# A fused attention and mixture-of-experts kernel: softmax sums turned in the products' PSUM bank, gathers released one by one, PSUM tiles for expert 0's pieces, and another order of ScalarE's copies

## The chip, the cores and the metric

The kernel runs on one core of a Trainium2 chip. Its time is the device time of one execution in microseconds, as the median of three runs. A profile of one more execution, taken by the hardware profiler, shows when each engine was busy and what it waited for.

## What is computed

Banded causal attention, whose output is at once the input of a layer of eight experts, of which each token uses one. All data is float32. Cut to what matters:

```python
B, H, S, D = 4, 8, 768, 64;  n_global, n_local = 8, 96
N, E, F = 3072, 8, 1024                     # tokens, experts, hidden size
scores = (q @ k.T) / sqrt(D) - slope[h] * dist    # dist: n_local for global keys outside the band
keep = (key < n_global) | ((0 <= query - key) & (query - key < n_local))
a = softmax(where(keep, scores, -1e9));  x = (a @ v) -> [3072, 512]
logits = x @ w_gate;  expert = argmax(logits);  gate = softmax(logits)[expert]
h = relu(x @ w1[expert]);  out = gate * (h @ w2[expert])   # 512 -> 1024 -> 512
```

## The kernel before

Each engine executes its instructions in the order in which the code calls them, and the instructions of different engines meet through semaphores. So the order of the calls in the loop at L803 is the schedule: if an instruction waits, everything behind it on its engine waits as well.

**Attention** (banded_attention, L370). The work is cut into 48 units: batch b, pair of heads j and a third c of the sequence, which is two blocks of 128 queries. A batch has 12 units. The loop at L803 takes two units in each step. scores (L486) multiplies blocks of 64 x 128 of the keys with the queries (L497) into a PSUM tile s of two banks; the keys of the block itself come from kT, and those of the block before it, with the eight global keys put in front, from kA. ScalarE takes the exponential (L503), and VectorE multiplies by a table of weights W that holds bias and mask (L510 for c = 0, L514 otherwise). One step later attend (L520) forms the products with v (L531) in the bank o_all; ScalarE copies them to w2_f (L534), and TensorE then forms the column sums of the exponentials with vectors of ones in the bank c_all (L553). Two steps after the scores turn (L556) transposes the products into px (L561), and ScalarE copies them into rows xr of the tokens (L566).

**PSUM.** The eight banks are handed out as follows: ps_s has two tiles of two banks (the scores), ps_o one bank (po_all, named o_all), ps_m two banks (tag m, everything small), ps_c one bank (pc_all, named c_all). A tile whose pool is full has to wait for the readers of the tile it takes the place of.

**For each pair of heads.** turn_qk (L448) transposes k and q on VectorE. keys_at (L419) makes kA with two ScalarE copies (L420, L422); the loop calls it at the end of the step of unit c = 1 for the next pair. turn_v (L441) makes va with two ScalarE copies (L444, L445); the loop calls it after unit c = 2, for the next pair. load and load_v start the DMAs some pairs ahead.

**For each batch, when its 12 units are through.** In the first step of the next batch (m = 0): sums_out (L572) copies the column sums to sums (L573), and partials (L586) forms partial logits for each pair of heads with products not yet divided by the sums (pl L592, ScalarE copy L594). In the second step (m = 2): recip_of (L575) transposes the sums (L578), adds them (two VectorE reductions, L581) and takes the reciprocals (L584); then logits (L596) transposes the partial logits into pq (L605, two tiles), and VectorE scales them by the reciprocals (L608), adds them over the heads and computes the gates. recip_of needs room in PSUM for the transposed sums: the loop takes the tile of the step's second unit early and puts them into its unused columns (the first lines below). In later steps spread (L628) ranks the tokens of each expert (VectorE, many small operations), finish_x (L620) multiplies the rows by the reciprocals (L624) and stores them to x_tok in DRAM (L245), tables (L657) builds one-hot tables (mv L662, oh L667), and spread_sum (L671) turns them into the lists of tokens by expert (pi L676). For batch 2, the last that is worked on inside the loop, all of this is packed into the steps m = 4 and m = 6.

```python
if b > 0 and n0 % nb == 2 and n == n0:
    st["ps"] = ps_s.tile([P, 2, 512], F32, tag="s", name=f"s_{n + 1}")
    recip_of(b - 1, st["ps"][:, :, 3 * P:4 * P])
...
if i == 0:
    while pending:
        gather_one(*pending.pop(0))
```

**Hand-over to expert 0.** Expert 0 starts before the last batch is finished, with 256 of its tokens from batches 0 to 2. half_0 (L684) prepares their list. fetch_0(0) (L693), called before the products of the last but one step, turns the list into rows (a matmul pw in rows_of, L263) and queues eight gathers on GpSimd (gather_one, L281, an indirect DMA of 32 rows each), all at once (the last lines above). Behind the loop (L858 on) comes a list written out by hand: sums, partial logits, logits, rows and tables of batch 3, with pieces of expert 0 in between (work, L726): early_hidden (L715, hidden_0: ph L339, relu L341) and early_result (L718, result_0: po L347, scaled by the gates into y on VectorE, L327). All early_hidden pieces share the two halves of one tile ph of ps_s, all early_result pieces the two halves of another, po. The half of ph that is not in use at first also holds the transposed sums of the last batch. turn_x (L289) transposes the gathered rows of a token block into xe on VectorE.

pace (L308) is the means by which gathers are spread over the experts' work: it takes the next gather from the list pending and makes it wait for a given instruction.

**Experts.** From L1198 on, hidden (L1115) and result (L1170) go through the experts: ph L1125, relu L1127, po L1182, then y L327 and an indirect DMA to the output. Weights come by SyncE's DMAs while the expert before is worked on.

Of the kernel before, what the change touches and what calls it, by code (L numbers as in the profile page):

```python
# [29 lines left out]
def kernel(  # L30
# [339 lines left out]
    def banded_attention():  # L370
        with ExitStack() as actx:
# [114 lines left out]
            def scores(n):  # L486
# [4 lines left out]
                ps = st.pop("ps") if "ps" in st else ps_s.tile([P, 2, 512], F32, tag="s", name=f"s_{n}")  # L491
# [11 lines left out]
                nc.scalar.activation(e[:, :, 0:w], ps[:, :, 0:w], AF.Exp, scale=D ** -0.5)  # L503
# [16 lines left out]
            def attend(*ns):  # L520

                for n in ns:
# [3 lines left out]
                    for t in range(2):  # L526
                        mine = [(m, own) for m, (u, own) in enumerate(bl) if u == t]
                        for m, own in mine:
                            i = 2 * c + t
                            for h in range(2):  # L530
# [3 lines left out]
                nc.scalar.copy(out=w2_f[:, o:o + 2 * P * len(ns)],  # L534
                               in_=po_all[:, ns[0] % 2:ns[-1] % 2 + 1, :, :].rearrange("p n t q -> p (n t q)"))
                for n in ns:
# [5 lines left out]
                    for own in (1, 0):  # L542

                        lots = [(1, 2)] if c == 0 and not own else [(0, 1), (1, 2)] if m == 1 and not own else [(0, 2)]
                        for t0, t1 in lots:
                            for h in range(2):
# [3 lines left out]
                                else:  # L550
# [3 lines left out]
                                                 start=(m == 0), stop=(m == nb - 1))  # L554

            def turn(n):  # L556
# [5 lines left out]
                for i in range(2):  # L562
# [3 lines left out]
                    nc.scalar.copy(out=xrs[b, c][:, :, P * j:P * j + P], in_=px[:, 2 * i:2 * i + 2, :])  # L566
# [8 lines left out]
            def recip_of(b, pr):  # L575

                for t in range(2):
                    nc.tensor.transpose(pr[:, t, :], sums[:, t, :], ident)  # L578
# [114 lines left out]
            def fetch_0(i):  # L693
# [6 lines left out]
                if i == 0:  # L700
                    while pending:
                        gather_one(*pending.pop(0))
                else:
                    for _ in range(2):
                        gather_one(*pending.pop(0))
                    plan(1)
# [8 lines left out]
            def early_hidden(z, f0):  # L715
                return hidden_0(st["ph"][:, f0 // 2 % 2, 0:2 * P], z, f0, 2)

            def early_result(z, f0):  # L718
                return result_0(st["po"][:, z, :], z, f0, 2, later)
# [76 lines left out]
            weights(0)  # L796
            nu = len(units)
# [5 lines left out]
            for n0 in range(0, nu, 2):  # L803
# [5 lines left out]
                for n in two:  # L809
# [8 lines left out]
                    if b > 0 and n0 % nb == 2 and n == n0:  # L818

                        st["ps"] = ps_s.tile([P, 2, 512], F32, tag="s", name=f"s_{n + 1}")  # L820
                        recip_of(b - 1, st["ps"][:, :, 3 * P:4 * P])
# [6 lines left out]
                if n0 >= 4:  # L828
                    turn(n0 - 4)
                    if b > 0 and m == 2:  # L830
                        logits(b - 1)
                    if n0 == nu - 4:
                        fetch_0(0)
                    attend(n0 - 2, n0 - 1)
                if b > 0 and m == 0:
                    sums_out(b - 1)
                    partials(b - 1)
                if b > 0 and m == 4:
                    spread(b - 1)
                if b > 0 and m == (4 if b == B - 1 else 8):  # L840
                    for i in range(NB // 2):
                        finish_x(b - 1, i)
                if 0 < b and m == (4 if b == B - 1 else 6):
                    tables(b - 1)
# [435 lines left out]
```

## Time and profile before

| | before |
|---|---|
| device time, three runs | 534.8, 536.1, 540.2 us |
| median | 536.09 us |
| the profiled execution | 538.75 us, span of the instructions 537.0 us |
| mean granted clock of TensorE in it | 0.985 of full speed |
| gathers (L281, xq) of expert 0 | 15, 1052 ns each |
| scores (L497) | 704 matmuls, 40.1 + 34.9 us |
| exponentials (L503) written to the tiles e | 36, 946 ns each |

The page of the profile gives the busy time and the number of instructions of each engine first: PE is the matrix multiplication of TensorE, PEld its load of weights, which overlaps with PE, DVE VectorE, ACT ScalarE, POOL GpSimd. Views of the trace answer closer questions: the waits of an engine (what it waited for, and who ended the wait), windows (busy time of each engine in a stretch of time), and the timeline (each instruction with its start, its duration, and in brackets the idle time of its engine before it and who ended that). In a timeline "s<-qT,kT" names the output tile and the inputs, "128x1024 f32" the partitions and elements, "x4" that four like instructions follow one another. An idle time in brackets ended by "remote" was ended by a semaphore whose sender the profile doesn't name.

### The profile page before, as it was taken

What the parts mean: (1) busy time and instruction counts of PE and PEld (TensorE: products, weight loads), DVE (VectorE), ACT (ScalarE), POOL (GpSimd) and SP (SyncE); (2) the same over time, 40 slices, a digit from 0 to 9 for tenths busy, and PEclk for the clock granted to TensorE, in tenths of its full rate; (3) what the DMA queues carried; (4) which work ended last, traced back from release to release, by engine and by line L of the source; (5) the groups of instructions that cost most, each with busy time, mean ns of one, the idle gap of its engine ahead of it and who ended that gap; (6) DMA issues with size and microseconds to landing.
All of it is one profiled execution on the core that took longest, in us unless ns stands there. A gap on an engine that the chain in (4) does not pass through costs nothing.

```text
span 537.0 us, 8730 instructions
## 1 busy us (share of the span) xinstructions
PE 502.6 (94%) x3476; PEld 322.0 (60%) x3476; DVE 176.3 (33%) x420; ACT 146.5 (27%) x288; POOL 137.3 (26%) x153
## 2 busy tenths in 40 slices
PE   4988998998986898999999999999999999999994
PEld 3875886885774773995445545545544855545541
DVE  4755796795873453131030021012002011021010
ACT  4886666666743210201101100100110101101100
POOL 5000000000014025655245225324304624411001
PEclk9999899899998999999999999999999999999997
DMA  9989599799591088195456183471554675301001
GB/s 156 165 141 163 98 181 222 140 175 235 113 310 35 6 221 257 43 240 187 109 125 204 24 182 106 144 180 62 175 114 103 209 157 151 109 21 38 1 21 39
DMA packets 145202, 72.00 MB, mean 134 GB/s; under 512 B 126688, under 2 KB 126694, under 8 KB 145152
## 3 DMA queue, kind: packets, MB, share of 16 engines
q1 hardware_dynamic: 137360, 58.16, 46.7%
q0 software_dynamic: 5264, 12.59, 7.7%
q10 hardware_dynamic: 2528, 0.59, 0.6%
q8 instruction: 29, 0.48, 0.4%
q14 instruction: 21, 0.17, 0.1%
HBM read 59.00 MB, written 12.75 MB: 134 GB/s over the span
## 4 chain that ended last, share of the span: by engine, by line
PE 84%; DVE 4%; ACT 3%; SPq 3%; DMA 1%; another core or an unknown queue 1%; issue 1%; ACTq 0%; POOL 0%; POOLq 0%; DVEq 0%
PE ph L1125 29%; PE po L1182 26%; PE o_all L531 6%; PE s L497 6%; PE c_all L553 4%; SPq L404 3%; PE ph L339 3%; PE po L347 2%; PE px L561 2%; PE po L1162 2%; PE pt L1191 1%; PE pl L592 1%; DMA w_second<-in_q_dram 1%; PE pi L676 1%
## 5 line engine op out<-in xcount | busy, mean ns | idle before, releaser
L1127 ACT ACTIVATE hT<-ph 128x416 f32<-128x416 f32 (+4 forms) x64 | 29.9, 468 | 279.8 <-PE ph L1125 195.3
L281 POOL DMA_INDIRECT xq_s<-x_tok,rows_s x72 | 72.6, 1008 | 55.5 <-ACT hT L1127 39.2
L1125 PE MATMUL ph<-xe,w_second 128*128 128x416 f32 (+3 forms) x256 | 79.4, 470 | 0.0
L327 DVE TENSOR_SCALAR y<-po,gslot_s 128x512 f32<-128x512 f32 (+1 forms) x17 | 12.8, 751 | 201.4 <-PE po L1182 201.4
L1125 PE MATMUL ph<-xe,w_first 128*128 128x208 f32 (+3 forms) x256 | 75.9, 457 | 1.0 <-DVE y L327 0.8
L1182 PE MATMUL po<-w_second,hT 128*128 128x512 f32 (+1 forms) x176 | 76.2, 592 | 0.0
L1125 PEld LDWEIGHTS ph<-xe,w_second 128*128 128x128 f32 x256 | 48.2, 190 | 29.4 <-issue 10.4
L1125 PEld LDWEIGHTS ph<-xe,w_first 128*128 128x128 f32 x256 | 47.4, 190 | 28.8 <-issue 10.3
L281 POOL DMA_INDIRECT xq<-x_tok,rows x15 | 15.8, 1052 | 182.3 <-DMA w_first<-in_moe_w_dram 150.3
L1182 PE MATMUL po<-w_first,hT 128*128 128x512 f32 (+1 forms) x144 | 62.3, 592 | 0.0
L1182 PEld LDWEIGHTS po<-w_second,hT 128*128 128x128 f32 (+1 forms) x176 | 33.2, 189 | 41.3 <-issue 40.7
L319 POOL DMA_INDIRECT out_dram<-y,idx_s x17 | 17.1, 1006 | 124.7 <-DVE xe L292 71.7
L1182 PEld LDWEIGHTS po<-w_first,hT 128*128 128x128 f32 (+1 forms) x144 | 27.2, 189 | 34.0 <-issue 33.5
L497 PE MATMUL s<-qT,kT 64*128 64x128 f32 x384 | 40.1, 291 | 7.7 <-DVE recips L581 6.8
L497 PE MATMUL s<-qT,kA 64*128 64x128 f32 x320 | 34.9, 297 | 3.5 <-ACT kA L422 3.5
L497 PEld LDWEIGHTS s<-qT,kT 64*128 64x128 f32 x384 | 30.9, 199 | 11.1 <-DVE recips L581 7.5
L514 DVE TENSOR_TENSOR e<-e,Wb 128x1024 f32<-128x1024 f32 x24 | 28.8, 1213 | 24.8 <-ACT e L503 24.8
L503 ACT ACTIVATE e<-s 128x1024 f32<-128x1024 f32 (+1 forms) x36 | 33.1, 946 | 9.2 <-PE s L497 7.0
L497 PEld LDWEIGHTS s<-qT,kA 64*128 64x128 f32 x320 | 25.8, 197 | 10.4 <-ACT kA L422 4.9
L531 PE MATMUL o_all<-e,vt 128*64 128x128 f32 x288 | 29.7, 284 | 0.7 <-issue 0.7
L531 PE MATMUL o_all<-e,va 128*64 128x128 f32 x240 | 25.4, 288 | 0.2 <-issue 0.2
L553 PE MATMUL c_all<-e,one_of 128*32 128x256 f32 (+1 forms) x304 | 21.7, 359 | 0.2
(202 smaller groups left out, 523.6 us busy)
## 6 DMA issues: line engine op xcount, KB each, us to landing
w_second<-in_moe_w_dram SPq DMA_DIRECT2D x16, 512.0 KB
w_second<-in_moe_w_dram SPq DMA_DIRECT2D x4, 2048.0 KB
x_tok<-xr SPq DMA_DIRECT2D x24, 256.0 KB
w_first<-in_moe_w_dram SPq DMA_DIRECT2D x12, 512.0 KB
w_first<-in_moe_w_dram SPq DMA_DIRECT2D x3, 2048.0 KB
vt<-in_v_dram SPq DMA_DIRECT2D x31, 192.0 KB
w_second<-in_q_dram SPq DMA_DIRECT2D x60, 96.0 KB
w_second<-in_k_dram SPq DMA_DIRECT2D x60, 96.0 KB
```

Of the source, the lines that this page charges most:

```text
L281: return nc.gpsimd.indirect_dma_start(out=xq[:, i, :], out_offset=None, in_=x_tok[0:NJ * top, :], in_offset=bass.IndirectOffsetOnAxis(ap=c ...
L319: p = nc.gpsimd.indirect_dma_start(out=to[:, :], out_offset=bass.IndirectOffsetOnAxis(ap=where, axis=0), in_=y[0:rows, :], in_offset=None, ...
L339: done = nc.tensor.matmul(ph[:, P * f:P * f + P], lhsT=w1_0[:, 0, kc, c0:c0 + P], rhs=xe_0[:, kc, P * q:P * q + P], start=(kc == 0), stop= ...
L404: nc.sync.dma_start(t[p0:p0 + 32, :, :], src[b, 2 * j + h].rearrange("(c t) d -> t c d", t=32)[:, :, 32 * d:32 * d + 32])
L497: nc.tensor.matmul(ps[:, h, P * m:P * m + P], lhsT=lhsT, rhs=qT[r, P * i:P * i + P], start=True, stop=True)
L503: nc.scalar.activation(e[:, :, 0:w], ps[:, :, 0:w], AF.Exp, scale=D ** -0.5)
L514: nc.vector.tensor_tensor(out=eh, in0=eh, in1=W[:, 2 * j:2 * j + 2, P:3 * P].rearrange("p h (o c) -> p h o c", o=1).to_broadcast([P, 2, 2, ...
L531: nc.tensor.matmul(po_all[D * h:D * h + D, n % 2, t, :], lhsT=vt[:, h, i, :] if own else va[:, h, i - 1, :], rhs=st[n][:, h, P * m:P * m + ...
L553: nc.tensor.matmul(pc[32 * g:32 * g + 32, t0:t1, :], lhsT=one_of[:, 31 - r:63 - r], rhs=rhs, start=(m == 0), stop=(m == nb - 1))
L1125: nc.tensor.matmul(ph[:, 0:C], lhsT=w1t[:, 0, kc, P * fc:P * fc + P], rhs=xe[:, kc, 0:C], start=(kc == 0), stop=(kc == KC - 1))
L1127: done = nc.scalar.activation(hT[:, fc, 0:C], ph[:, 0:C], AF.Relu)
L1182: nc.tensor.matmul(po[0:rows, :], lhsT=hT[:, fc, P * q:P * q + rows], rhs=w2t[:, 0, fc, :], start=(fc == 0), stop=(fc == FC - 1))
```

## The change

It has five parts.

1. recip_of puts the transposed sums into the products' bank (po_all) and not into a tile of the scores. It is called a step earlier, right behind partials, and behind the partials of the last batch likewise. The early tile st["ps"] goes.
2. fetch_0(0) no longer issues its eight gathers but leaves them in pending, and is called inside attend, between the copy of the products and the column sums. Behind every exponential, every copy of the products (at the end of attend) and every copy of turn stands a call of pace(1, ...), which takes one gather from pending if there is one and makes it wait for that instruction. pending is empty in the attention but for the stretch behind fetch_0(0): so, in the order of the calls, one gather waits for the products' copy of units 42 and 43, two for the exponentials of units 46 and 47, two for the copies of turn(42), one for the products' copy of units 44 and 45, two for the copies of turn(44).
3. Each piece of early_hidden takes a ps_s tile of its own; early_result uses the products' bank for the first token block and the column sums' bank for the second.
4. ScalarE's copies: from the third step on the next pair's keys (keys_at) come ahead of the products' copy; turn_v of a pair comes at the end of the step of its own unit c = 0 and not after unit c = 2 of the pair before.
5. Batch 2's tables come ahead of its finish_x. In the tail the transposes of the second block of xq come behind the logits and turn(nu - 2), and ahead of finish_x(B - 1, 0); before, they came ahead of all this.

```diff
@@ -488,7 +488,7 @@
                 w = P * len(bl)
-                ps = st.pop("ps") if "ps" in st else ps_s.tile([P, 2, 512], F32, tag="s", name=f"s_{n}")
+                ps = ps_s.tile([P, 2, 512], F32, tag="s", name=f"s_{n}")
                 for m, (t, own) in enumerate(bl):
@@ -500,7 +500,7 @@
                     e = ep.tile([P, 2, 512], F32, tag="e", name=f"e_{n}")
-                nc.scalar.activation(e[:, :, 0:w], ps[:, :, 0:w], AF.Exp, scale=D ** -0.5)
+                pace(1, nc.scalar.activation(e[:, :, 0:w], ps[:, :, 0:w], AF.Exp, scale=D ** -0.5))
                 if n == 0:
@@ -517,7 +517,7 @@
-            def attend(*ns):
+            def attend(*ns, between=None):
@@ -531,8 +531,10 @@
                 o = 2 * P * (ns[0] % nb)
-                nc.scalar.copy(out=w2_f[:, o:o + 2 * P * len(ns)],
+                done = nc.scalar.copy(out=w2_f[:, o:o + 2 * P * len(ns)],
                                in_=po_all[:, ns[0] % 2:ns[-1] % 2 + 1, :, :].rearrange("p n t q -> p (n t q)"))
+                if between:
+                    between()
                 for n in ns:
@@ -552,6 +554,7 @@
                                                  start=(m == 0), stop=(m == nb - 1))
+                pace(1, done)
@@ -563,7 +566,7 @@
                         xrs[b, c] = xrp.tile([P, 2, DM], F32, tag="xr", name=f"xr_{b}_{c}")
-                    nc.scalar.copy(out=xrs[b, c][:, :, P * j:P * j + P], in_=px[:, 2 * i:2 * i + 2, :])
+                    pace(1, nc.scalar.copy(out=xrs[b, c][:, :, P * j:P * j + P], in_=px[:, 2 * i:2 * i + 2, :]))
@@ -572,8 +575,9 @@
-            def recip_of(b, pr):
+            def recip_of(b):
+                pr = po_all[:, 0, :, :]
                 for t in range(2):
@@ -697,10 +701,7 @@
                         pending.append((xq_0[h], rows_0[i][:, TB * h:TB * h + TB], k, N - S if i == 0 else N))
-                if i == 0:
-                    while pending:
-                        gather_one(*pending.pop(0))
-                else:
+                if i > 0:
                     for _ in range(2):
@@ -713,10 +714,12 @@
             def early_hidden(z, f0):
-                return hidden_0(st["ph"][:, f0 // 2 % 2, 0:2 * P], z, f0, 2)
+                ph = ps_s.tile([P, 2, 512], F32, tag="s", name=f"ph_0_{z}_{f0}")
+                return hidden_0(ph[:, 0, 0:2 * P], z, f0, 2)
             def early_result(z, f0):
-                return result_0(st["po"][:, z, :], z, f0, 2, later)
+                po = (po_all, pc_all)[z].rearrange("p n t q -> p (n t q)")
+                return result_0(po, z, f0, 2, later)
@@ -794,6 +797,13 @@
             weights(0)
+            def next_keys(two):
+                for n in two:
+                    pr, c = divmod(n, NB // 2)
+                    if c == 1 and pr + 1 < B * NJ:
+                        keys_at(*pairs[pr + 1][1:3], 0, NB - 1)
             nu = len(units)
@@ -815,10 +825,6 @@
                         attend(n - 2)
-                    if b > 0 and n0 % nb == 2 and n == n0:
-                        st["ps"] = ps_s.tile([P, 2, 512], F32, tag="s", name=f"s_{n + 1}")
-                        recip_of(b - 1, st["ps"][:, :, 3 * P:4 * P])
                     if n == 2:
@@ -827,31 +833,34 @@
                     turn(n0 - 4)
+                    next_keys(two)
                     if b > 0 and m == 2:
                         logits(b - 1)
-                    if n0 == nu - 4:
-                        fetch_0(0)
-                    attend(n0 - 2, n0 - 1)
+                    attend(n0 - 2, n0 - 1, between=(lambda: fetch_0(0)) if n0 == nu - 4 else None)
                 if b > 0 and m == 0:
...
                     partials(b - 1)
+                    recip_of(b - 1)
                 if b > 0 and m == 4:
                     spread(b - 1)
-                if b > 0 and m == (4 if b == B - 1 else 8):
+                if 0 < b < B - 1 and m == 8:
                     for i in range(NB // 2):
...
                     tables(b - 1)
+                if b == B - 1 and m == 4:
+                    for i in range(NB // 2):
+                        finish_x(b - 1, i)
                 if 0 < b and m == (6 if b == B - 1 else 8):
...
                     half_0(0)
+                if n0 < 4:
+                    next_keys(two)
                 for n in two:
                     pr, c = divmod(n, NB // 2)
-                    if c == 1 and pr + 1 < B * NJ:
-                        keys_at(*pairs[pr + 1][1:3], 0, NB - 1)
-                    if c == 2 and pr + 1 < B * NJ:
-                        turn_v(pr + 1)
+                    if c == 0 and pr > 0:
+                        turn_v(pr)
                     if c == 1 and pr + 2 < B * NJ:
@@ -859,16 +868,15 @@
             turn_x(xe_0, xq_0[0], TB)
-            turn_x(xe_0[:, :, P:2 * P], xq_0[1], TB)
             while weights_0:
                 weights_0.pop(0)()
-            st["ph"], st["po"] = (ps_s.tile([P, 2, 512], F32, tag="s", name=f"{i}_0") for i in ("ph", "po"))
-            recip_of(B - 1, st["ph"][:, 1, 2 * P:4 * P].rearrange("p (t q) -> p t q", t=2))
             work(1)
             partials(B - 1)
+            recip_of(B - 1)
             work(1)
...
             turn(nu - 2)
+            turn_x(xe_0[:, :, P:2 * P], xq_0[1], TB)
             finish_x(B - 1, 0)
...
```

## The prediction

> **What bounds the kernel now.** I read the page first, then TensorE's waits, then the stages in 10 us windows, then the timeline at each gap. The page's first part:
>
> ```profile
> span 537.0 us, 8730 instructions
> PE 502.6 (94%) x3476; PEld 322.0 (60%) x3476; DVE 176.3 (33%) x420; ACT 146.5 (27%) x288; POOL 137.3 (26%) x153
> ```
>
> TensorE is the bound: it stands still for 34.4 us in all, and some 7 us of that lie behind the last matmul. No edit here takes work from TensorE, so only its idle time, and time in which it runs slowly, can be won. From 215 us on (the experts) it is at 10.00 of 10 us in almost every window; what can be won lies in the attention and in the hand-over to expert 0. TensorE's waits (engine, tile and line waited for: us in total, times, longest):
>
> ```profile
> PE s L497 <- DVE recips L581: 6.8, 3, 2.3
> PE s L497 <- ACT kA L422: 3.5, 2, 2.0
> PE px L561 <- ACT w_second L534: 3.2, 1, 3.2
> PE ph L339 <- ACT hT L341: 0.9, 2, 0.5
> PE pi L676 <- DVE oh L667: 0.8, 1, 0.8
> PE ph L1125 <- DVE y L327: 0.8, 1, 0.8
> PE po L347 <- DVE y L327: 0.8, 1, 0.8
> PE pw L263 <- DVE gslot L691: 0.7, 1, 0.7
> ```
>
> Every one of these is touched by the change. The windows (us; busy of PE, PEld, DVE, ACT, POOL; clock; DMA share; GB/s) show a second price, a lower clock after a gap:
>
> ```profile
> 50.00:60.00 10.00, 7.75 (x88) 6.23 (x88) 5.47 (x14) 4.32 (x10) 0.00 (x0) 0.83 0.80 147
> 90.00:100.00 10.00, 7.71 (x90) 6.05 (x86) 6.12 (x18) 4.55 (x10) 0.00 (x0) 0.83 1.01 186
> 130.00:140.00 10.00, 7.29 (x106) 5.84 (x106) 6.35 (x19) 5.04 (x11) 0.00 (x0) 1.00 0.90 170
> 160.00:170.00 10.00, 5.79 (x56) 2.94 (x52) 3.97 (x9) 3.09 (x5) 6.91 (x7) 0.99 0.21 57
> ```
>
> The first three are the starts of batches 1 to 3. The timeline of the first (start, duration, work, idle before it and who ended it):
>
> ```profile
> 50.93 0.44 PE L578 MATMUL s<-ident,w_second 128*128 128x128 f32 x2
> 52.10 1.22 DVE L514 TENSOR_TENSOR e<-e,Wb 128x1024 f32<-128x1024 f32 x1 [3.46 <-ACT e L503]
> 53.25 0.31 DVE L581 TENSOR_REDUCE recips<-s 128x24 f32<-128x48 f32 x2
> 53.62 0.79 PE L497 MATMUL s<-qT,kT 64*128 64x128 f32 x4 [2.25 <-DVE recips L581]
> ```
>
> The sums are turned (L578) into spare columns of the tile of the next scores; those scores wait until VectorE has read them, and VectorE has a product of 1.22 us ahead of that. The fourth window is another thing: eight gathers run on GpSimd one behind the other, and ScalarE and TensorE lose their pace.
>
> ```profile
> 161.95 1.00 POOL L281 DMA_INDIRECT xq<-x_tok,rows  x1 [0.30 <-issue]
> 164.28 1.02 ACT L503 ACTIVATE w_second<-s 128x1024 f32<-128x1024 f32 x1 [1.85 <-remote]
> 164.53 2.38 PE L553 MATMUL c_all<-e,one_of 128*32 128x256 f32 x16
> 169.50 0.59 ACT L534 COPY w_second<-o_all 128x512 f32<-128x512 f32 x1 [3.65 <-remote]
> 170.14 1.12 PE L561 MATMUL px<-ident,w_second 128*128 128x128 f32 x4 [3.23 <-ACT w_second L534]
> ```
>
> Sixteen c_all matmuls take 2.38 us here and 1.06 us elsewhere (59.09 us); the copy at 169.50 waits for products whose last matmul started at 164.30.
>
> **What the Trainium skill says.** TensorE: Matmul & The Clock Gate, Part 1: an idle TensorE is throttled to half its clock and gets it back after some 3.4 us of work. The trace agrees: 0.83 over 10 us is 3.4 us at half, after gaps of 2.25 and 2.3 us, though not after the third, equal gap. PSUM — Partial Sum Buffer, PSUM bank collisions raise a hardware error: two engines have to be kept apart by bank, not by address; this is why scores that write other columns still wait (2.25 us) for the readers of the sums, and why a tile in another bank frees them. The first page, Engine queue depths: ScalarE takes its instructions strictly in order; in the trace a copy va L444 that waits 2.36 us for its DMA (27.94) holds the exp behind it until 29.23. Perfetto Trace Analysis, GPSIMD Engine Instruction: time GpSimd by start-to-start spacing; here gathers follow at 1.30 us (160.64, 161.95, 163.25).
>
> **The change part by part.**
>
> *Sums in the products' bank* (L575, L821, L866). The two transposes (0.44 us) stay, but come right behind the partial logits (L592), into a bank whose reader (L534, done at 48.38) and source (L573, done at 48.68) are ready before those end at 49.9. VectorE stood idle for 3.46 us there, so the two reductions and the reciprocal (0.31 + 0.45) are hidden. The wait of the scores goes. What takes its place: the second pq tile (L605) needs the xr copies (L566), which are behind both exps, and ScalarE now has turn_v (0.73 + 0.62 = 1.35) ahead of the exps. ScalarE: 50.43 end of L594, +1.35 turn_v, +0.94 and +0.80 exps, +0.65 xr = 54.2. TensorE: 49.9, +0.44 transposes, +1.76 scores, +0.59 px, +0.49 pq = 53.2, so it waits 1.0 us, and after 0.44 more it starts the products (L531) at 54.6, against 57.41. Saved: 2.8 us, a us of it from the half clock. The same offset of 4.7 us behind the end of L592 gives 94.5 against 96.74 in batch 2 and 134.4 against 136.18 in batch 3: 2.2 and 1.8. Sum **6.8 us**, bounds 5 and 8.5 (all waiting and slow clock gone).
>
> *ScalarE's order* (turn_v a unit later, next keys ahead of the products' copy). At 33.53 the scores waited 1.48 us for kA L422, which was late because of the 2.36 us stand for the DMA of v. A unit later that v has landed. I take **1.2**, bounds 0 and 1.5; the 2.0 us wait at 12.29 is not touched. Elsewhere ScalarE's two units cost some 4.5 us of TensorE's 5.3 us, so an order does not show.
>
> *Batch 2's tables ahead of its x* (L840): VectorE's order of finish_x (3 x 1.17) and tables is turned round, so oh is ready 3.5 us sooner and the 0.8 us wait goes. The rows' matmul (pw, 0.7 us wait) now stands between products and sums and finds its input ready. But VectorE is busy without a break from 135 to 154 us, and its e of unit 43 has about 1.2 us to spare at 155.68. I take **1.0** of the 1.5.
>
> *Tiles of expert 0's own* (L715 to L719, L865). Gone: 0.5 and 0.4 us at the last sums (175.58, 176.43), 0.9 before ph L339, 0.8 before po L347, 0.8 before ph L1125: 3.4. Added on VectorE's path: the four transposes of xq's second half (4 x 0.31 = 1.25) now stand between the logits and x, so oh comes 1.25 us later, and pi L676, which had nothing to spare once TensorE is faster, waits some 1.1. The last gather's transposes end at 210.7 against a start of L1125 at 214.95: enough slack. Net **2.0**, bounds 1 and 3.
>
> *Gathers one by one*. From 158.35 (scores of the last two units) to 175.1 TensorE takes 16.8 us. The same rows at full pace: scores 1.99, px 0.59, products and sums 2.9, px 0.59, again 2.9: 9.0. So the stretch loses 7.8 us. Each gather now waits for one ScalarE instruction; GpSimd has nothing else queued behind it, and the first four are needed only by expert 0's first piece. Whether the eight gathers as a burst cause the stall is not shown by this trace: bounds 0 and 7.8. The measured times run from 534.8 to 540.2, and the profiled execution took 538.75, 2.7 above the median, so I count the stall as 5.1 us in a median run and take **4.0** off: less crowded, but GpSimd's own spacing of 1.3 us still puts gathers 3 to 8 close together.
>
> Sum: 6.8 + 1.2 + 1.0 + 2.0 + 4.0 = 15.0; 536.1 - 15.0 = **521.1 us**.
>
> **Rivals.** *The stall stays* (27%): six of the eight gathers still lie back to back in the same stretch of small matmuls; 536.1 - 11.0 = 525. Against: the burst is broken up at its start. *It goes altogether* (14%), and the median had all of its 7.8: 536.1 - 11.0 - 7.8 = 517. *VectorE or ScalarE takes over* (10%): both were at 8.5 to 9 of 10 us in the windows 60 to 80 and 100 to 120, and less idle TensorE makes these denser; half of the 11 us is kept, no stall is won: 530.5. *Slower* (7%): ScalarE's queue is in order, so keys (0.92 us) ahead of the products' copy in some 15 pairs, of which TensorE might feel each as a wait for o_all, cost 13.8; with half of the rest lost as well, 536.1 + 13.8 - 5.5 = 544. Against: o_all is next written more than 3 us after that copy.
>
> **The numbers.** My forecast has 42%. The range, 515.5 to 530, holds it and the first two rivals (83%). Faster by over 1% (below 530.7) are these and half of the third: 0.88. Within 1%: the other half, 0.05. Slower: 0.07.
>
> **What would show it.** Right: no wait of s L497 for recips; about a us of wait of pq L605 for xr at each of three batch starts; clock 1.00 in the windows around 50 and 90 us; no wait of L347 and L1125 for y; pi L676 waits about 1 us for oh in the last batch alone; GpSimd's first gathers at uneven spacing. Wrong: the stretch of the last two units still takes 15 us or more (the stall is not the burst's); TensorE waits for ACT w_second L534 in many units (the order of ScalarE's copies hurts); the page's DMA rows keep VectorE waiting for k.

## The result, and the profile after

| | before | after |
|---|---|---|
| device time, median of four runs each | 537.72 us | 517.38 us |
| runs | 534.8, 536.09, 539.35, 540.2 | 517.02, 517.28, 517.47, 519.9 |
| ratio | | 0.963, 95% interval 0.958 to 0.969 |

The changed kernel is 20.3 us faster against these four runs, 18.7 against the median of 536.09 that the prediction started from. The forecast was 521.1 us in a range of 515.5 to 530; the time lies inside it, 3.7 us below the forecast.

The traces are of executions of 538.75 and 519.9 us. The page's first part, after:

```profile
span 518.2 us, 8738 instructions
PE 494.7 (95%) x3476; PEld 318.7 (62%) x3476; DVE 175.7 (34%) x420; ACT 145.8 (28%) x288; POOL 137.0 (26%) x153
```

The 3476 matmuls are the same, and the span is 18.8 us shorter. TensorE's busy time falls by 7.9 us, since it runs less at half clock and at a slow pace, and its idle time by 10.9 us. TensorE's waits after (engine, tile and line waited for: us in total, times, longest):

```profile
PE s L497 <- ACT kA L422: 4.5, 3, 2.0
PE pq L609 <- ACT xr L569: 1.7, 2, 0.9
PE pq L609 <- DMA w_second<-in_k_dram: 0.9, 1, 0.9
PE pi L680 <- DVE oh L671: 0.7, 1, 0.7
```

The scores no longer wait for recips, 6.8 us before. The new wait of pq for the copies xr is there, 0.9 us at each of three batch starts (one of the three is put down to a DMA). No piece of expert 0 waits for y or for recips, and pi waits for oh once, in the last batch. The windows that answer to those of before (us; busy of PE, PEld, DVE, ACT, POOL; clock; DMA share; GB/s), and one more:

```profile
40.00:50.00 10.00, 8.37 (x104) 6.37 (x100) 6.26 (x6) 7.42 (x15) 0.00 (x0) 0.83 0.94 163
50.00:60.00 10.00, 9.14 (x133) 7.13 (x126) 6.83 (x19) 6.63 (x13) 0.00 (x0) 1.00 0.83 151
90.00:100.00 10.00, 9.15 (x139) 7.15 (x137) 9.59 (x21) 6.76 (x15) 0.00 (x0) 1.00 0.96 175
150.00:160.00 10.00, 9.71 (x148) 7.19 (x148) 4.70 (x9) 6.54 (x13) 6.27 (x6) 1.00 0.66 230
```

The starts of batches 1 and 2 run at full clock. The window from 40 us has a half clock that before did not have: a wait of 1.63 us for kA. In the last window six of the eight gathers lie (POOL 6.27), and TensorE is at 9.71 of 10 us, where before it was at 5.79 in the window with the gathers (160 to 170).

To see where the time went I cut each trace at three points that every variant has: the start of the first scores (L497) of unit 12, which is the first of batch 1, that of unit 46, and the first relu of expert 0 (L341). "Batch starts" is the sum of the distances between the first scores of units 12 and 16, 24 and 28, 36 and 40, a part of the third column. "The stretch" is the time from the scores of unit 46 to the relu.

| us in the trace | start to unit 12 | unit 12 to 46 | of it batch starts | the stretch: unit 46 to first relu | first relu to end | span |
|---|---|---|---|---|---|---|
| before | 42.7 | 115.7 | 50.5 | 20.2 | 358.5 | 537.0 |
| after | 40.7 | 110.2 | 44.4 | 11.2 | 356.1 | 518.2 |

These cuts are TensorE's, because TensorE is the bound. The recorded expectations below count from ScalarE's exponentials (L503) instead, so they give 17.1 us for the stretch of before. All fourteen traces take the same 22.8 us from unit 16 to 24 and from unit 28 to 36: nothing is won or lost there.

The largest single piece, 9.0 of the 18.8 us, is the short stretch ahead of expert 0's first relu. It is the piece for which the prediction had only a guess at the cause, so the experiments begin there.

### The profile page after: what moved, and what is told of

The parts are those of the page before. It is cut to its first block, busy times and chain, and to the rows that moved or that the text cites. A ratio compares the mean times of both kernels' runs of the same rounds, so it can differ in the third digit from the quotient of the medians.

```text
span 518.2 us, 8738 instructions
## 1 busy us (share of the span) xinstructions
PE 494.7 (95%) x3476; PEld 318.7 (62%) x3476; DVE 175.7 (34%) x420; ACT 145.8 (28%) x288; POOL 137.0 (26%) x153
## 4 chain that ended last, share of the span: by engine, by line
PE 82%; DVE 5%; ACT 4%; SPq 3%; DMA 3%; issue 1%; POOL 0%; POOLq 0%; DVEq 0%; ACTq 0%
PE ph L1133 30%; PE po L1190 27%; PE s L497 6%; PE o_all L531 5%; PE c_all L555 3%; PE po L1170 2%; DMA vt<-in_v_dram 2%; PE ph L339 2%; SPq L404 2%; PE pt L1199 1%; PE px L564 1%; PE o_all L347 1%; PE c_all L347 1%; ACT e L503 1%; PE pi L680 1%
## 5 line engine op out<-in xcount | busy, mean ns | idle before, releaser
L1133 PEld LDWEIGHTS ph<-xe,w_first 128*128 128x128 f32 x256 | 47.4, 190 | 27.7 <-issue 10.8
L1190 PEld LDWEIGHTS po<-w_second,hT 128*128 128x128 f32 (+1 forms) x176 | 33.2, 189 | 41.3 <-issue 40.7
L319 POOL DMA_INDIRECT out_dram<-y,idx_s x17 | 17.1, 1005 | 125.1 <-DVE xe L292 72.1
L497 PE MATMUL s<-qT,kT 64*128 64x128 f32 x384 | 39.6, 290 | 1.7 <-ACT qT L438 0.9
L497 PE MATMUL s<-qT,kA 64*128 64x128 f32 x320 | 35.0, 298 | 4.5 <-ACT kA L422 4.5
L503 ACT ACTIVATE e<-s 128x1024 f32<-128x1024 f32 (+1 forms) x36 | 33.3, 944 | 12.6 <-PE s L497 12.4
L497 PEld LDWEIGHTS s<-qT,kT 64*128 64x128 f32 x384 | 31.0, 200 | 4.5 <-ACT kA L422 1.7
L497 PEld LDWEIGHTS s<-qT,kA 64*128 64x128 f32 x320 | 26.2, 200 | 9.5 <-ACT kA L422 5.7
L531 PE MATMUL o_all<-e,vt 128*64 128x128 f32 x288 | 27.7, 275 | 0.0
L531 PE MATMUL o_all<-e,va 128*64 128x128 f32 x240 | 24.2, 280 | 0.1
L555 PE MATMUL c_all<-e,one_of 128*32 128x256 f32 (+1 forms) x304 | 20.6, 359 | 0.0
```

The lines of the kernel that those rows point to most:

```text
L319: p = nc.gpsimd.indirect_dma_start(out=to[:, :], out_offset=bass.IndirectOffsetOnAxis(ap=where, axis=0), in_=y[0:rows, :], in_offset=None, ...
L497: nc.tensor.matmul(ps[:, h, P * m:P * m + P], lhsT=lhsT, rhs=qT[r, P * i:P * i + P], start=True, stop=True)
L503: pace(1, nc.scalar.activation(e[:, :, 0:w], ps[:, :, 0:w], AF.Exp, scale=D ** -0.5))
L531: nc.tensor.matmul(po_all[D * h:D * h + D, n % 2, t, :], lhsT=vt[:, h, i, :] if own else va[:, h, i - 1, :], rhs=st[n][:, h, P * m:P * m + ...
L555: nc.tensor.matmul(pc[32 * g:32 * g + 32, t0:t1, :], lhsT=one_of[:, 31 - r:63 - r], rhs=rhs, start=(m == 0), stop=(m == nb - 1))
L1133: nc.tensor.matmul(ph[:, 0:C], lhsT=w1t[:, 0, kc, P * fc:P * fc + P], rhs=xe[:, kc, 0:C], start=(kc == 0), stop=(kc == KC - 1))
```

## Experiments

All times are medians against runs of the kernel before on the same chip. The kernels came in three groups of four, each on another chip, where the kernel before had medians of 536.8, 535.6 and 535.8 us. The kernel after was timed once, at 517.4 us, on a chip that is not on record and beside a median of 537.7 for the kernel before. So a difference to the kernel after of some 2 us or less can be the chip's.

**Is it the burst of gathers, or late instructions of TensorE?** Four kernels. The second part of the change alone, in the kernel before:

```diff
-                    if n0 == nu - 4:
-                        fetch_0(0)
-                    attend(n0 - 2, n0 - 1)
+                    attend(n0 - 2, n0 - 1, between=(lambda: fetch_0(0)) if n0 == nu - 4 else None)
...
-                    while pending:
-                        gather_one(*pending.pop(0))
+                pace(1, nc.scalar.activation(e[:, :, 0:w], ps[:, :, 0:w], AF.Exp, scale=D ** -0.5))
...
+                pace(1, done)
```

> The kernel before with the second part of the change alone: the eight gathers of expert 0 released one by one behind ScalarE's instructions, and their list of rows made inside attend. Theory 1 (eight gathers issued as one burst slow TensorE down): the stretch from the scores of units 46 and 47 to the first relu of expert 0 shrinks from 17.1 us (161.41 to 178.52) to about 10, and the time falls by 6 to 8 us, to 528 to 531. Theory 2 (TensorE's own instructions come late, because their refill stands behind the 2 MB of expert 0's second weights on busy DMA queues; the gathers have no part in it): the stretch stays at 15 us or more and the time within 2 us of the kernel before.

Measured: 537.4 against 536.8 us, ratio 1.001 (1.000 to 1.002). The gathers one by one bring nothing, although TensorE keeps its pace in this trace. The reverse, in the kernel after:

```diff
+                    while pending:
+                        gather_one(*pending.pop(0))
```

> The kernel after with its second part undone: the list of rows ahead of attend and all eight gathers at once, as before; all else as after. Theory 1: the stall comes back, 6 to 8 us more than the kernel after, some 524. Theory 2: within 2 us of the kernel after (517.4), unless the refill happens to fall late again.

Measured: 517.8 us, within 0.4 of the kernel after; its stretch takes 10.8 us. So the gain that theory 1 forecast fails to appear both ways. The third and fourth kernel moved the gathers, and the weights that share the DMA queues with them:

```diff
             turn(nu - 4)
+            fetch_0(0)
             attend(nu - 2, nu - 1)
```

> The kernel before with the list of rows and the burst of eight gathers moved one step later, behind turn of units 44 and 45. Theory 1: the slow stretch moves with the burst, so it begins some 5 to 8 us later, and the scores, products and sums of units 44 to 47 run at full pace; the time stays about the same. Theory 2: the slow stretch stays at about 160 to 170 us, whatever the gathers do.

```diff
-                    if n % 3 > 0 and n >= 18:
+                    if n % 3 > 0 and n >= 18 and len(weights_0) > FC:
...
-                weights_0.pop(0)()
+                behind(weights_0.pop(0)(), turned, "the weights come later")
```

> The kernel before with the eight loads of expert 0's second weights (2 MB, on the queues from 152 to 162 us) held until the last copy of turn for units 44 and 45. The burst of gathers stays where it was. Theory 1: the stall stays, the time within 2 us of the kernel before. Theory 2: TensorE's refill finds free queues, the stall goes, and the time falls by 6 to 8 us.

Measured: 540.6 us (ratio 1.008, 1.006 to 1.011) and 540.3 us (1.008, 1.005 to 1.011). Both are slower, which neither theory had, and neither trace has a slow stretch at 160 to 170 us; nor have the other two of this group. So these traces cannot tell what slows TensorE, but they show that the time does not fall where it keeps its pace, and neither theory explains that. What they show in its place is a third thing. The timeline of the variant with late gathers, VectorE first, then TensorE (start, duration, work, idle before it and who ended that):

```profile
174.88 0.31 DVE L292 STREAM_TRANSPOSE xe<-xq 128x128 f32<-128x128 f32 x1 [0.99 <-DMA xq<-x_tok,rows]
176.14 0.31 DVE L292 STREAM_TRANSPOSE xe<-xq 128x128 f32<-128x128 f32 x1 [0.95 <-DMA xq<-x_tok,rows]
176.37 0.28 DVE L581 TENSOR_REDUCE recips<-ph 128x24 f32<-128x48 f32 x2
```

```profile
167.16 0.44 PE L578 MATMUL ph<-ident,w_second 128*128 128x128 f32 x2 [0.49 <-ACT w_second L573]
176.71 3.78 PE L339 MATMUL ph<-xe,w_first 128*128 128x128 f32 x16 [9.11 <-DVE recips L581]
```

TensorE turned the last sums at 167.16, into the tile ph. The reductions that read them (L581) stand in VectorE's queue behind the transposes of all eight gathers, so they start only at 176.37, when the last gather has landed. The first piece of expert 0 writes the same tile and waits 9.11 us; after that gap its 16 matmuls take 3.78 us at half clock and not 2.05. The variant with late weights has the same wait, 7.84 us: its gathers now share the queues with 2 MB of weights and land late. Its last gather is issued at 168.07 and taken by VectorE at 175.29. And the variant with the gathers one by one waits 4.54 us there:

```profile
172.00 3.78 PE L339 MATMUL ph<-xe,w_first 128*128 128x128 f32 x16 [4.54 <-DVE recips L584]
```

The piece and the sums lie in different halves of the tile, one bank each, so it is the shared tile and not a shared bank that makes TensorE wait. So in the kernel before two things lay side by side: in the execution that the prediction read, TensorE was slow until 170 us, and VectorE's queue was held until 170.2 us by the gathers. By these traces, taking one of the two away leaves the other to hold the end.

**Theory 3: VectorE's queue.** If that is so, it should be enough to take the second four transposes out of the way, or the sums out of the tile. The order alone, in the kernel before:

```diff
             turn_x(xe_0, xq_0[0], TB)
-            turn_x(xe_0[:, :, P:2 * P], xq_0[1], TB)
...
             turn(nu - 2)
+            turn_x(xe_0[:, :, P:2 * P], xq_0[1], TB)
             finish_x(B - 1, 0)
```

> The kernel before with one edit: VectorE's transposes of the second block of gathered rows (gathers 5 to 8) come behind the logits and turn of units 46 and 47, and no longer ahead of the last batch's sums. Theory 3 (VectorE's queue: the reductions of the last sums stand behind those transposes, these wait for the last gather, and the first piece of expert 0 shares its tile with the sums, so TensorE waits for the eighth gather): with gathers released one by one TensorE stood 4.5 us before that piece and then ran it at half clock, 3.8 us and not 2.05; both go, some 1 us comes back in front of pi, so the time falls by 4 to 6 us, to 531 to 533. Theory 4 (the gain in that stretch comes from the PSUM tiles of expert 0's own or from the sums' new bank, not from VectorE's order): within 1.5 us of the kernel before.

Measured: 536.0 against 535.6 us, ratio 1.000 (0.998 to 1.003). The expected gain is not there. In its trace the wait for recips is down to 0.4 us, but the stretch still takes 17.5 us:

```profile
171.98 0.37 ACT L573 COPY w_second<-c_all 128x256 f32<-128x256 f32 x1 [1.61 <-remote]
```

```profile
172.41 0.69 PE L578 MATMUL ph<-ident,w_second 128*128 128x128 f32 x2 [2.43 <-ACT w_second L573]
173.51 3.78 PE L339 MATMUL ph<-xe,w_first 128*128 128x128 f32 x16 [0.41 <-DVE recips L581]
```

The last c_all matmuls were over at 169.98 and ScalarE's copy of the sums started only at 171.98, the transposes behind it waited 2.4 us, and the first piece ran at half clock all the same. That loss is the slow issue of before in another place (TensorE or ScalarE starts its next instruction late though the trace shows nothing that it waits for), and is taken up below; what the order would give without it, this run does not show. The same edit taken back in the kernel after:

```diff
             turn_x(xe_0, xq_0[0], TB)
+            turn_x(xe_0[:, :, P:2 * P], xq_0[1], TB)
...
             turn(nu - 2)
-            turn_x(xe_0[:, :, P:2 * P], xq_0[1], TB)
```

> The kernel after with only that edit undone: the transposes of the second block come ahead of the last batch's sums again. Theory 3: the sums no longer share a tile with expert 0's pieces, so no piece waits for them; only the scaled logits do, and the last gather (about 165 us) is there about when they are due: within 1.5 us of the kernel after, so either edit alone frees TensorE. Rival: the order alone carries the whole gain, and the time goes up by 4 us or more.

Measured: 519.5 us, 2.1 more than the kernel after, and no wait for recips. Theory 3 had at most 1.5. The stretch takes 13.7 us and not 11.2, by slow issue again; the part behind the first relu is 0.7 us shorter. The direct test of the theory leaves the gathers out:

```diff
-                    while pending:
-                        gather_one(*pending.pop(0))
+                    pending.clear()
```

> The kernel before without the first eight gathers of expert 0: VectorE transposes rows of zeros, so the first 256 tokens of expert 0 get no result; all else is the same work. Theory 3 (the last gather, through VectorE's queue, sets when expert 0's first piece may start): nothing waits there any more, the stretch from the scores of units 46 and 47 to the first relu shrinks from about 17 us to about 11, and the time falls by 5 to 6 us against the kernel before, to 530 to 531. If the slow issue of TensorE at 160 to 170 us is tied to gathers in flight it can't occur, and the runs lie within 1.5 us of each other; if it has another cause, it occurs here too, with TensorE's instructions at a third of their pace in that stretch, and the time stays above 533.

Measured: 530.7 against 535.8 us, ratio 0.991 (0.988 to 0.993): the 5 us that theory 3 expected. The stretch takes 12.2 us (11.0 from the exponential, as expected). Its timeline:

```profile
163.86 1.66 DVE L292 STREAM_TRANSPOSE xe<-xq 128x128 f32<-128x128 f32 x8
169.08 0.32 DVE L581 TENSOR_REDUCE recips<-ph 128x24 f32<-128x48 f32 x2 [3.56 <-PE ph L578]
```

```profile
169.46 2.05 PE L339 MATMUL ph<-xe,w_first 128*128 128x128 f32 x16 [0.42 <-DVE recips L581]
```

The eight transposes run in a row, VectorE waits for TensorE and not the other way round, and the piece starts 0.42 us behind the sums at full clock. The 13 runs lie between 529.9 and 532.9 us, wider than the 1.5 us expected, but closer together than those of the kernel before beside it, which lie between 533.0 and 538.8 with one more at 541.1.

**The sums' bank.** Alone in the kernel before (the early tile, and the call of recip_of ahead of expert 0's first piece, go):

```diff
+                pr = po_all[:, 0, :, :]
...
                     partials(b - 1)
+                    recip_of(b - 1)
...
             partials(B - 1)
+            recip_of(B - 1)
```

> The kernel before with the first part of the change alone: the sums turned in the products' bank a step earlier, those of the last batch too. The prediction's step: 6.8 us less at the three batch starts. Undone in the kernel after, the same part cost 12.4 us. If its worth depends on the other parts, it gives 5 to 8 us here; if the 12 us are its own, 11 to 13. In the last batch the first piece of expert 0 no longer waits for the reductions of the sums, since these lie in another bank, so by theory 3 some 5 us come on top of the 6.8: about 12 us, 524.

Measured: 523.1 against 535.8 us, 12.7 less, ratio 0.977 (0.972 to 0.982), near the 12 that theory 3 expected, of which the prediction's step has 6.8. The trace divides it. The batch starts take 41.5 us in place of 50.2 in the trace without gathers, so 8.7. The stretch takes 13.9 and not 18.1 as in the trace with the gathers one by one, so 4.2, although VectorE's transposes still stand ahead of the reductions and TensorE has slow issue here:

```profile
161.99 2.05 PE L339 MATMUL ph<-xe,w_first 128*128 128x128 f32 x16
163.98 1.50 PE L593 MATMUL pl<-w_second,wg_sb 128*32 128x384 f32 x16
165.40 0.44 PE L579 MATMUL o_all<-ident,w_second 128*128 128x128 f32 x2
165.68 1.95 PE L339 MATMUL ph<-xe,w_first 128*128 128x128 f32 x16
```

```profile
165.95 0.32 DVE L582 TENSOR_REDUCE recips<-o_all 128x24 f32<-128x48 f32 x2 [2.91 <-PE o_all L579]
```

Two things changed at once for the last batch. The first piece now stands ahead of the transposes of the sums in TensorE's order, so it has nothing to wait for in any tile. The second piece stands behind them and starts 0.27 us before the reductions: this one shows what the sums' own place is worth. Which of the two, the order or the place, carries the 4.2 us was not tested apart. Taken back for the batch starts in the kernel after:

```diff
+                        st["ps"] = ps_s.tile([P, 2, 512], F32, tag="s", name=f"s_{n + 1}")
+                        recip_of(b - 1, st["ps"][:, :, 3 * P:4 * P])
```

> The kernel after with the sums of batches 0 to 2 turned in the spare columns of a scores tile again, in the step with m = 2; the last batch's sums stay in the products' bank. The prediction's step: 6.8 us more than the kernel after, 524.2; by the distances between exponentials in the trace of the variant with the burst back (15.60 to 14.33, 16.68 to 14.34 and 15.63 to 14.32 us at the three batch starts) 4.9 us more, 522.3.

Measured: 529.7 us, 12.4 more than the kernel after. The waits for recips are 8.5 us, and the batch starts take 52.1 us, 11.1 more than in the variant with the burst (40.9). In the new order ScalarE has turn_v ahead of the exponentials at just this place, so VectorE gets its products, and after them the reductions, later still: TensorE waits up to 2.8 us and not 2.3, and runs at half clock behind all three waits, where the trace before did so behind two. The stretch takes 13.6 us, 2.4 more than after. The two make 13.5, a little more than measured.

**Own tiles, and ScalarE's order,** each taken back in the kernel after:

```diff
-                ph = ps_s.tile([P, 2, 512], F32, tag="s", name=f"ph_0_{z}_{f0}")
-                return hidden_0(ph[:, 0, 0:2 * P], z, f0, 2)
+                return hidden_0(st["ph"][:, f0 // 2 % 2, 0:2 * P], z, f0, 2)
...
-                return result_0(po, z, f0, 2, later)
+                return result_0(st["po"][:, z, :], z, f0, 2, later)
```

> The kernel after with the pieces of expert 0 in the halves of two shared tiles again. The prediction's step: waits of 0.9 (ph for relu), 0.8 (po for y) and 0.8 us (ph of the experts for y) come back, so 2 to 2.5 us more than the kernel after, 519.5 to 520. If the tiles do more than that, as theory 4 has it, 4 us or more.

Measured: 522.3 us, 4.9 more. From the first relu to the end the trace has 358.7 us and not 356.1, so 2.7 us, the three waits that the prediction named (TensorE's waits of this variant):

```profile
PE ph L339 <- ACT hT L341: 0.9, 2, 0.5
PE ph L1132 <- DVE y L327: 0.8, 1, 0.8
PE po L347 <- DVE y L327: 0.8, 1, 0.8
```

Another 2.4 us are again in the stretch, 13.6 us.

```diff
                     turn(n0 - 4)
-                    next_keys(two)
...
-                if n0 < 4:
-                    next_keys(two)
+                next_keys(two)
-                    if c == 0 and pr > 0:
-                        turn_v(pr)
+                    if c == 2 and pr + 1 < B * NJ:
+                        turn_v(pr + 1)
```

> The kernel after with ScalarE's copies in the order of before: the next pair's keys at the end of the step, behind the products' copy, and v's copies after unit c = 2 of the pair before. The prediction's step: 1.2 us more (0 to 1.5), 518.6. If the wait of 1.48 us at 33.5 us was the DMA's and not the order's, no difference.

Measured: 521.2 us, 3.8 more. 2.4 of it is the stretch once more (13.6 us). The other 1.4 us lie ahead of unit 40: its first scores start at 130.7 us, and at 129.3 in half_back. In the first batch TensorE waits for kA again, a wait that no trace with the new order has at this place:

```profile
34.44 0.49 PE L497 MATMUL s<-qT,kA 64*128 64x128 f32 x4 [1.34 <-ACT kA L422]
```

The batch starts hardly differ, 41.5 us in the old order and 41.0 in half_back. ScalarE's timeline of the kernel after at the start of batch 1 shows what the new order costs there:

```profile
50.30 1.10 ACT L598 COPY w_second<-pl 128x384 f32<-128x384 f32 x2 [0.31 <-PE pl L596]
51.29 0.73 ACT L444 COPY va<-vt 128x640 f32<-128x640 f32 x1
52.05 0.62 ACT L445 COPY va<-vt 16x512 f32<-16x512 f32 x1
52.58 1.02 ACT L503 ACTIVATE e<-s 128x1024 f32<-128x1024 f32 x1
```

Two copies of va, 1.35 us, stand between the partial logits and the exponential, and TensorE then waits 0.9 us for the copies xr behind these, against 0.7 in the old order.

**A further step.** The kernel after with two more edits:

```diff
+                    if i0 == 0 or b == B - 1:
                         pq = ps_m.tile([P, i1 - i0, NJ, 32], F32, tag="m", name=f"pq_{b}_{i0}")
+                    else:
+                        pq = pc_all[:, b % 2, :, :].rearrange("p i (j w) -> p i j w", w=32)
...
-            finish_x(B - 1, 0)
...
             tables(B - 1)
-            for i in range(1, NB // 2):
+            for i in range(NB // 2):
```

> The kernel after with two more edits of its own kind. For batches 0 to 2 the second tile of turned partial logits (pq) goes into the half of the column sums' bank that is free then, so it no longer waits for the copies xr to empty one of the two small tiles: three waits of 0.86 us in the trace, 2.6 us. In the tail the first finish_x of the last batch comes behind the tables, so the one-hot table is ready 1.2 us earlier and the wait of 0.75 us of pi goes. Expected 3.3 us less than the kernel after, 514; if ScalarE or VectorE is then the bound at the batch starts, 516 to 517.

Measured: 518.6 us, 1.2 more than the kernel after. In the trace the first edit does win something: the three waits of pq are gone, a wait of c_all for VectorE's reading of pq has come, 1.2 us in all, and the batch starts take 39.2 us against 40.9 in the variant with the burst. The wait of pi is gone too, but the part from the first relu to the end is 356.1 us as before, so it was not what held that part. The stretch takes 13.6 us, 2.4 more than after, which hides the gain. Whether the kernel would be faster than the kernel after on one and the same chip was not tried; of the medians on record, that of the kernel after is the lowest.

**What stays open: TensorE's slow issue.** In the traces of half_back, tiles_back, sums_back, scalar_order_back and logits_bank the stretch takes 13.6 to 13.7 us, in those of the kernel after and of burst_back 11.2 and 10.8. TensorE and ScalarE in half_back:

```profile
157.21 1.63 PE L339 MATMUL ph<-xe,w_first 128*128 128x128 f32 x11
159.55 0.62 PE L339 MATMUL ph<-xe,w_first 128*128 128x128 f32 x4 [0.70 <-issue]
160.97 0.27 PE L339 MATMUL ph<-xe,w_first 128*128 128x128 f32 x1 [0.81 <-issue]
```

```profile
160.28 0.59 ACT L534 COPY w_second<-o_all 128x512 f32<-128x512 f32 x1 [5.19 <-issue]
```

TensorE issues its matmuls haltingly though nothing is waited for, and ScalarE's copy of products that were over at 155.5 us starts at 160.28. It is the picture of before at 160 to 170 us. In half_back and in the trace of before it ends (161.2 and 170.1 us) when the last gather has landed (VectorE takes it at 161.59 and 170.24), in sums_alone some 4 us earlier. It was absent, with the narrow spread of runs, where the gathers were left out; but the five traces with gathers and without it (gathers_alone, burst_back, gathers_late, w2_late, the kernel after) hold bursts as well as gathers one by one. So gathers as such are not enough for it, and a burst is neither needed nor enough. Where it occurs, a burst makes it no worse either: sums_alone, with the burst, takes 13.9 us for the stretch, the five with the gathers one by one 13.6 to 13.7.

What divides the traces best is something that no edit varied: the chip. None of the four traces of the first group has slow issue, and all seven traces with gathers of the other two groups have it. The chip of the traces before and after is not on record. No kernel was traced on two chips, so it stays open whether the chip is the cause, and what else it takes. For the parts taken back in the second and third group it means that some 2.4 us of each of those times are slow issue and not the part.

## Why the prediction came out as it did

The time lies inside the range, and the gain is 3.7 us larger than forecast. Most steps were right in mechanism; one was wrong in cause. That the sum comes out near is in part luck: the term for the gathers stands where a wait belongs that the prediction took for small.

- **Gathers one by one, 4.0 us: wrong.** The step took the stretch's loss of 7.8 us and put some of it down to the burst. The part is worth 0.6 us the other way alone and 0.4 us undone, nothing that can be told from no change. The loss was real in the trace before: from the scores of units 46 and 47 to the end of the last column sums it takes 16.7 us. But that part takes 8.8 us after and 8.8 to 8.9 in all four traces of the first group, two of which (gathers_late and w2_late) hold no part of the change. So no part of the change was shown to remove slow issue. What the change won in the stretch, 18.1 to 11.2 us between the traces of gathers_alone and after, both without slow issue, goes with the sums of the last batch. The prediction had noted that the burst as the cause was not shown by the trace, and kept 0 as a bound.
- **Tiles and sums of the last batch, 2.0 us net: right in mechanism, one term too small.** The three waits for relu and y cost 2.7 us undone, against 2.5 listed. The wait at the last sums was taken at its face value, 0.5 and 0.4 us. In that trace TensorE arrived so late that the wait was short; without TensorE's delay (gathers_alone) it is 4.5 us, with half clock behind it, 6.3 us in all. This is where most of the unlisted gain lies, and the sum comes out near because this term replaces the one for the gathers.
- **Sums in the products' bank, 6.8 us: right in mechanism, a little too small.** 8.7 us at the batch starts alone, just above the upper bound of 8.5, and 11.1 undone, where ScalarE's new order makes the old place worse. The wait that takes its place was forecast at 1.0 us and is 0.9; the products were to start 4.7 us behind the partial logits and start 4.4 us behind them (pl ends at 123.78, the products at 128.16).
- **ScalarE's order, 1.2 us: right.** Undone it costs 1.4 us, and the wait for kA in the first batch is the one that the step named. That v would have landed a unit later did not always hold: in the trace after, ScalarE still stands 3.18 us for its DMA, until 38.38, and TensorE waits 1.63 us for the kA behind it.
- **Tables ahead, 1.0 us: about right,** but not undone on its own. From unit 40 to 46 the trace without gathers takes 19.5 us and that of scalar_order_back 18.4, which have old and new places of the tables; 1.1 us, with other parts in it. The waits for oh (0.8) and of pw (0.7) of before are gone there; with the list of rows back in its old place (burst_back) pw waits 1.2 us.
- **pi L680** waits 0.7 us, forecast 1.1; from the first relu to the end half_back is 0.7 us shorter than the kernel after, which fits the cost of the four transposes on VectorE's path, taken as 1.25.
- **Rivals.** The first (the stall stays) is not in the trace after; five of its variants have slow issue and pay some 2.4 us for it. The second, 517 us with the stall gone altogether, gave the measured time, but by way of the burst, which is not the cause. The third (VectorE or ScalarE takes over) is in the trace in small: the wait of pq for ScalarE at the batch starts. The fourth (slower by the order of the keys) is not: TensorE has no wait for w_second L534 after.

Summed from the traces: 8.7 (batch starts) + 1.4 (ScalarE) + 1.1 (tables) + 6.9 (the stretch) + 2.0 (behind the relu, 2.7 less 0.7) = 20.1 us, against 18.7 to 20.3 measured.

## What to carry to other kernels

When two delays lie side by side, a trace shows the one that ends last, and the wait behind it looks short: ask for each in-order queue what stands ahead of the instruction that frees a shared tile, and when that would have been ready if the visible delay were gone. A shared PSUM tile turns such a queue into a wait of TensorE, and another tile, or a place ahead of the shared one in TensorE's order, frees it without touching the queue. Cut a trace at the instructions of the engine that is the bound: by ScalarE's exponentials scalar_order_back seems to lose 2.9 us in the first batch and to win 2.8 at the batch starts against burst_back, since copies of va stand ahead of a batch's first exponential there; by TensorE's scores it loses 0.9 and 0.6. And measure a part alone as well as undone: here 12.7 and 12.4 us for one part, but made of different pieces (8.7 and 4.2; 11.1 and slow issue).

## What the runs showed of the hardware beyond what was expected

- After an idle stretch of 1.63 us TensorE ran at half clock (scores of 0.65 us for four matmuls and not 0.39, from 42.87 us in the trace after). The Trainium skill, TensorE: Matmul & The Clock Gate, Part 1, puts the drop behind an idle window of some 3.4 us; the measurement decides here, and shows that a gap of half that can be enough. The other three runs of this kernel are 2.4 us and more shorter than the one traced; whether it was this wait that they lacked, their times alone do not say.
- The slow issue of TensorE described above, with ScalarE's copy of the products starting 4.7 us after these were over (half_back), in eight of the fourteen traces; all eight have gathers in flight, and the trace without them has none of it.
- GpSimd issued most gathers 1.30 us apart whether or not each waits for a ScalarE instruction: 160.64, 161.95, 163.25 before, and 156.90, 158.20, 159.50, 160.80, 162.10 in the kernel after, behind first gaps of 1.50 and 1.89. Releasing them one by one changed their start, hardly their spacing.
